# Layer two of a routed MLP behind an FFT convolution: products of the high halves first, gate factors earlier, rows of pairs fetched earlier

## The chip, the cores and the metric

The kernel runs on one core of a Trainium2 chip. The metric is device time in microseconds (us), from the launch to the end on that core; times of several executions are given with their median. A profile is one further execution, recorded by the hardware. The engines are TensorE (PE, with its weight loads as PEld), VectorE (DVE), ScalarE (ACT), GpSimd (POOL) and SyncE (SP). In this kernel SP issues nearly all transfers, and POOL issues the indirect ones that scatter rows.

## What is computed

The reference takes 8 sequences of 2496 rows of 256 numbers, convolves each with a filter by FFT (forward transform, product with the filter, inverse transform), and passes each of the 19968 resulting rows to one of 8 experts:

```
Y = irfft(rfft(x, axis=1) * F)            # 8 x 2496 x 256
logits = rows @ w_gate                    # 19968 x 8
e = argmax(logits);  g = softmax(logits)[e]
out[row] = g * (relu(row @ w1[e]) @ w2[e])   # 256 -> 1024 -> 256
```

## The kernel before

**First half.** The transforms are matrix products in fp32 in small pieces (`forward1`, `spec1`, `spec2`, `filt_`, `join`, `spec3`, `inv1`, `inv2`). For each sequence `route1` to `route6` find expert, gate and place in memory of every row, and POOL scatters the rows into `xs`, a table in device memory sorted by expert (`inv3`). Beside that the experts' weights are scaled and split into two fp16 halves, high and low, and kept in device memory as `wscr` (`w_load` to `w_out`; `w_max` is a DVE reduction of freshly loaded fp32 weights `wf`).

**Second half.** Rows are taken from `xs` in blocks of 128 of one expert. Blocks come in three stages: 7 pairs (the program's unit is a pair of blocks), 63 pairs, and single blocks. For a unit `load` fetches the rows into `xb` (4 buffers), `prep` finds the scale of each row on DVE, `split` makes the high half on ACT and the low half on DVE (both `xs`), and `turn` lets SP issue a DMA transposition into `xt` (2 buffers). `layer1` multiplies by the first weights (`wa`) into the PSUM tile `ph`; ACT makes the activation `hs` and its high half `hh`, `halves` makes the low half `hl` on DVE. `layer2` multiplies `hh` and `hl` by the second weights (`wb`) into the PSUM tile `po`, of which there is one buffer; `out_` multiplies by the gate factor `g` on ACT and `send` scatters the result. Numbers are split, so each product is three matmuls: high by high, high by low, low by high.

The weights of a unit lie in one of a few slots (`wa0`, `wa1`, `cm`, `T1` for the first layer, `wb0`, `wb1`, `bm`, `ff2` for the second; `cm`, `bm`, `T1`, `ff2` are tiles of the first half that are used again, and the views name them `cm`, `bm`, `T`, `ff`). The 63 pairs use two slots in turn. `loadw` issues about 1 MB for each unit and layer under a condition: only if the unit's expert differs from that of the slot's last unit does it move anything, at the first two pairs and at seven more. In the trace an issue that moves data takes 0.33 us or more on SP, one that is skipped 0.1 us.

**Order of the work.** Every piece is put on a list with a key, `at(key, function, ...)`; the list is sorted by key and executed, and each piece appends its instructions to the engines' queues. So a key is no time: it only sets the order in which each engine takes its instructions, and every engine then works down its own queue and waits where it must. In the pair stages a block is `d` long in keys and a pair `u = 2 d` (1.0 in the stage of 63). For a pair whose first layer starts at key z the lines at 1241 to 1253 say

```
at(max(opened(s), z - (2.1 * u if m > 1 else 2.0), OPEN + 0.1), load, k)
...
    y = max(opened(s) + 0.3, z - (2.1 if b0 < 2 else 1.35 * u if m > 1 else 1.4)) + 0.4 * d * q
    at(y, prep, b0 + q)
    at(y + 0.1, split, b0 + q)
    at(y + 0.15, turn, b0 + q)
```

where q is 0 for the pair's first block and 1 for its second. `loadw` of the first layer comes at z - 1.24 and of the second at z - 0.01, each after the slot's last reader.

Of the kernel before, what the change touches and what calls it, by code (L numbers as in the profile page):

```python
# [9 lines left out]
F32 = mybir.dt.float32  # L10
# [135 lines left out]
def tile_fft_moe(ctx, tc, x, filt_r, filt_i, w_gate, w1, w2, cst, out):  # L146
    nc = tc.nc
# [59 lines left out]
    with ExitStack() as fctx:  # L207
# [716 lines left out]
        for b in range(B):  # L924
# [5 lines left out]
            for i, f in enumerate(  # L930
# [12 lines left out]
            ):  # L943
                at(s0 + v * RT[i], f[0], b, *f[1:])
            lead = 3.2 if b < B - 2 else 2.0 if b < B - 1 else 1.3
# [25 lines left out]
        for q in range(2 * E):  # L971
            e, i = divmod(q, 2)
            z = K["w"] + K["wp"] * q
            at(z - 2.25, w_load, e, i)
            for d, f, *a in (
# [189 lines left out]
        def layer2(b, i):  # L1165
            k, j = home[b]
            m = units[k][2]
            w = wb[slot[k]]
            if i == 0:
                st[b] = (mps[2].tile([128, D], F32, name=f"po{b}", tag="pO"), *st[b][1:])  # L1170
            ps = st[b][0]
            wv = w[:, 0:4096].rearrange("p (i f d) -> p i f d", i=2, d=D)
            for f in range(4 * i, 4 * i + 4):
                c, e = divmod(f, 4 // m)
                o = (e * m + j) * 128
                for n, (q, r) in enumerate(((0, 0), (0, 1), (1, 0))):
                    nc.tensor.matmul(  # L1177
                        ps,
                        lhsT=hid[k, c][q][:, o : o + 128],
                        rhs=wv[:, r, f],  # L1180
                        start=(f == 0 and n == 0),
                        stop=(f == 7 and n == 2),
                    )
            if i:
                g0 = st[b][1]
                g = mps[0].tile([128, 1], F32, name=f"g{b}", tag="g", bufs=3)
                nc.vector.tensor_tensor(g, g0, w[:, 4096:4098].bitcast(F32), op=ALU.mult)
                st[b] = (ps, g, st[b][2])

# [47 lines left out]
        for k in range(nu):  # L1237
            s, i, m, b0 = units[k]
            z, d, _ = tau[b0]
            u = d * m  # L1240
            at(max(opened(s), z - (2.1 * u if m > 1 else 2.0), OPEN + 0.1), load, k)
            old = [j for j in range(k) if slot[j] == slot[k]]
# [6 lines left out]
            for q in range(m):  # L1249
                y = max(opened(s) + 0.3, z - (2.1 if b0 < 2 else 1.35 * u if m > 1 else 1.4)) + 0.4 * d * q  # L1250
                at(y, prep, b0 + q)
                at(y + 0.1, split, b0 + q)
                at(y + 0.15, turn, b0 + q)
            z, p = span(k)
# [72 lines left out]
```

## Time and profile before

| | us |
|---|---|
| median of 3 runs (lowest to highest) | 1317.54 (1315.71 to 1318.96) |
| the profiled execution, its own time | 1322.67 |
| its span, first to last instruction | 1320.8 |
| PE busy | 1295.3 (98%) |
| PE weight loads busy | 1116.5 (85%) |
| ACT busy | 825.7 (63%) |
| DVE busy | 748.8 (57%) |
| POOL busy | 368.2 (28%) |
| mean granted PE clock | 0.995 of full speed |

The chain that ended last runs through PE for 85% of the span and through transfers for 6%. The first half fills the span to about 450 us, the pairs run from there to about 1190 us, the single blocks to the end. Busy time is counted from the records of instructions; overlapping ones count once.

### The profile page before, as it was taken

The page shows a single profiled execution, that of the slowest core. Times are in us where ns is not written, and L with a number is a line of the kernel's source. Part 1 is how long each engine was busy: PE and PEld are TensorE (multiplying, and loading weights), DVE is VectorE, ACT ScalarE, POOL GpSimd, SP SyncE. Part 2 cuts the span into 40 slices and gives each one's busy share as a digit, 9 for nine tenths or more (in the row PEclk, how much of TensorE's full clock was granted, in tenths as well). Part 3 has the DMA queues.
Part 4 walks back from the last instruction along what each step waited for, and adds up shares of the span by engine and source line. Part 5 has one row for each costly group of instructions (what it writes and reads, how often), then busy time and mean ns, then how long its engine had stood idle before and what let it go on. Part 6 is the DMA issues. An engine that isn't in the chain of part 4 may idle for free.

```text
span 1320.8 us, 34604 instructions
## 1 busy us (share of the span) xinstructions
PE 1295.3 (98%) x12703; PEld 1116.5 (85%) x12703; DVE 748.8 (57%) x2408; ACT 825.7 (63%) x1539; POOL 368.2 (28%) x393
## 2 busy tenths in 40 slices
PE   8999999999999999999999999999999999999998
PEld 6887878878876778888888888888888888889997
DVE  2686776867866564555555545555555555544452
ACT  3566767767665676666666656666666666565564
POOL 5005345444345335422111111111211211121121
PEclk9999999999999999999999999999999999999999
DMA  8756656575636435762344342252253256548964
GB/s 216 207 149 224 204 179 224 170 232 166 202 125 190 96 94 141 216 131 74 83 115 105 106 102 77 74 137 77 74 149 78 75 139 153 144 120 231 289 164 141
DMA packets 167072, 193.99 MB, mean 147 GB/s; under 512 B 105341, under 2 KB 141785, under 8 KB 159220
## 3 DMA queue, kind: packets, MB, share of 16 engines
q1 hardware_dynamic: 146308, 147.15, 41.5%
q0 software_dynamic: 20592, 44.60, 10.8%
q8 instruction: 101, 1.65, 0.5%
q14 instruction: 71, 0.58, 0.2%
HBM read 255.61 MB, written 61.56 MB: 240 GB/s over the span
## 4 chain that ended last, share of the span: by engine, by line
PE 85%; DMA 6%; DVE 3%; issue 2%; ACT 2%; SPq 1%; POOL 0%; POOLq 0%; DVEq 0%; ACTq 0%
PE ph L1146 29%; PE po L1177 28%; PE py L696 6%; PE pi L419 5%; PE px L374 5%; PE f L289 5%; PE pg L681 3%; PE pt L356 2%; DMA xt<-xs 2%; PE plw L544 1%; DMA x<-in_x_dram 1%; DMA xb<-xs 1%; DMA ff<-in_filt_r_dram 1%; SPq L274 0%; ACT hs L1154 0%
## 5 line engine op out<-in xcount | busy, mean ns | idle before, releaser
L1162 DVE TENSOR_TENSOR hl<-hs,hh 128x512 f16<-128x512 f32 x322 | 222.0, 690 | 373.3 <-ACT hh L1156 361.2
L180 POOL DMA_INDIRECT out_dram<-ot,t x150 | 146.1, 974 | 632.5 <-ACT ot L1197 618.6
L1177 PEld LDWEIGHTS <-hh 128*128 128x128 f16 x2576 | 251.3, 98 | 34.4 <-issue 5.5
L180 POOL DMA_INDIRECT xs<-yt,dest x176 | 182.2, 1035 | 305.8 <-ACT T L298 80.3
L1154 ACT ACTIVATE hs<-ph 128x512 f32<-128x512 f32 x322 | 191.4, 594 | 80.3 <-PE ph L1146 72.6
L1156 ACT CAST hh<-hs 128x512 f16<-128x512 f32 x322 | 199.0, 618 | 10.3
L1146 PE MATMUL ph<-xt,cm 128*128 128x256 f16 (+1 forms) x1776 | 192.3, 265 | 2.5 <-DMA xt<-xs 1.3
L1146 PE MATMUL ph<-xt,T 128*128 128x256 f16 (+1 forms) x1728 | 188.2, 266 | 3.3 <-DMA xt<-xs 2.7
L1177 PE MATMUL po<-bm,hh 128*128 128x256 f16 x1104 | 184.8, 273 | 0.6 <-ACT ot L1197 0.6
L1146 PEld LDWEIGHTS <-cm 128*128 128x128 f16 x1776 | 163.8, 98 | 21.0 <-issue 3.5
L1177 PE MATMUL po<-ff,hh 128*128 128x256 f16 x1072 | 179.2, 273 | 0.0
L1146 PEld LDWEIGHTS <-T 128*128 128x128 f16 x1728 | 159.7, 98 | 22.0 <-issue 4.5
L1109 ACT ACTIVATE xs<-xb,s 128x256 f16<-128x256 f32 x161 | 81.7, 508 | 126.0 <-DVE s L1099 118.5
L1177 PE MATMUL po<-bm,hl 128*128 128x256 f16 x552 | 150.5, 273 | 0.0
L1177 PE MATMUL po<-ff,hl 128*128 128x256 f16 x536 | 146.1, 273 | 0.0
L1177 PEld LDWEIGHTS <-hl 128*128 128x128 f16 x1288 | 126.1, 98 | 14.6
L1197 ACT ACTIVATE ot<-po,g 128x256 f32<-128x256 f32 x150 | 71.1, 474 | 104.5 <-PE po L1177 81.2
L289 PEld LDWEIGHTS f<-a,x 117*128 117x128 f32 (+1 forms) x704 | 88.6, 195 | 16.5 <-issue 9.8
L289 PE MATMUL f<-a,x 117*128 117x117 f32 (+1 forms) x704 | 98.2, 282 | 1.6 <-issue 1.4
L391 DVE TENSOR_TENSOR tr<-px,ff 128x512 f32<-128x512 f32 x80 | 54.8, 684 | 78.9 <-PE px L374 61.8
L1110 DVE SCALAR_TENSOR_TENSOR xs<-xb,s,xs 128x256 f16<-128x256 f32 x161 | 77.5, 481 | 25.4 <-ACT xs L1109 25.4
L429 ACT COPY U<-pi 128x256 f32<-128x256 f32 (+1 forms) x160 | 55.2, 407 | 54.7 <-PE pi L419 54.7
(183 smaller groups left out, 1736.0 us busy)
## 6 DMA issues: line engine op xcount, KB each, us to landing
bm<-wscr SPq DMA_DIRECT2D x37, 1040.0 KB
cm<-wscr SPq DMA_DIRECT2D x37, 1024.0 KB
ff<-wscr SPq DMA_DIRECT2D x36, 1040.0 KB
T<-wscr SPq DMA_DIRECT2D x36, 1024.0 KB
xb<-xs SPq DMA_DIRECT2D x161, 130.0 KB
wb<-wscr SPq DMA_DIRECT2D x18, 1040.0 KB
wa<-wscr SPq DMA_DIRECT2D x18, 1024.0 KB
wf<-in_moe_w_dram SPq DMA_DIRECT2D x32, 512.0 KB
```

What stands on the lines that cost most here:

```text
L180: nc.gpsimd.indirect_dma_start(out=dst, out_offset=bass.IndirectOffsetOnAxis(ap=idx, axis=0), in_=src, in_offset=None, bounds_check=bound, ...
L289: nc.tensor.matmul(ps[:, n : n + m], lhsT=xt.pop((u, g))[:m], rhs=a1[:m, :m], start=True, stop=True,)
L374: nc.tensor.matmul(ps[64 * a : 64 * a + 64, i, j], lhsT=bm[:, 4 * it + 2 * j + i, 64 * a : 64 * a + 64], rhs=z[:, kk], start=True, stop=True,)
L696: nc.tensor.matmul(ps[:GP].rearrange("p g d -> p (g d)"), lhsT=dm, rhs=gt[:GP].rearrange("p g d -> p (g d)"), start=True, stop=True,)
L1109: nc.scalar.activation(xs_[:, 0], xb[:, :D], AF.Copy, scale=sc)
L1110: nc.vector.scalar_tensor_tensor(xs_[:, 1], xb[:, :D], sc, xs_[:, 0], op0=ALU.mult, op1=ALU.subtract)
L1146: nc.tensor.matmul(ps[:, n * f : n * f + n], lhsT=w[:, p : p + 128], rhs=xt[:, r, c, o1 : o1 + n], start=(a == 0), stop=(a == 5),)
L1154: nc.scalar.activation(s, ps, AF.Relu, scale=1.0 / B23)
L1156: nc.scalar.copy(hh, s)
L1162: nc.vector.tensor_tensor(hl, s, hh, op=ALU.subtract)
L1177: nc.tensor.matmul(ps, lhsT=hid[k, c][q][:, o : o + 128], rhs=wv[:, r, f], start=(f == 0 and n == 0), stop=(f == 7 and n == 2),)
L1197: nc.scalar.activation(ot, ps, AF.Copy, scale=g)
```

## The change

The diff does five things. `layer2` issues, for each half of its eight column groups, first the eight products with `hh` and then the four with `hl`, where before they alternated two and one. The gate factor `g` is formed at the start of a block's layer two instead of at its end, and the last block's result is put into a `ph` buffer instead of the only `po` buffer. In the stage of 63 pairs rows are fetched at z - 2.5 instead of z - 2.1, and the splitting and transposing of a block move closer behind its `prep` (keys y + 0.08 and y + 0.09 for the first block of a pair, y + 0.03 and y + 0.04 for the second, instead of y + 0.1 and y + 0.15). Where the pairs begin, the keys of units 0 and 1, of block 4 and of one routing step of the last sequence are set by hand. And the first fp32 weights are loaded at key 4.85, ahead of the constants at 4.9, instead of at 5.75.

```diff
--- before.py
+++ after.py
@@ -941,7 +941,7 @@
                     (route6,),
                 )
             ):
-                at(s0 + v * RT[i], f[0], b, *f[1:])
+                at(s0 + v * RT[i] - (0.15 if b == B - 1 and i == 1 else 0.0), f[0], b, *f[1:])
             lead = 3.2 if b < B - 2 else 2.0 if b < B - 1 else 1.3
 
 
@@ -971,7 +971,7 @@
         for q in range(2 * E):
             e, i = divmod(q, 2)
             z = K["w"] + K["wp"] * q
-            at(z - 2.25, w_load, e, i)
+            at(4.85 if q < 1 else z - 2.25, w_load, e, i)
             for d, f, *a in (
                 (-0.1, w_max, 0),
                 (0.1, w_max, 1),
@@ -1167,25 +1167,30 @@
             m = units[k][2]
             w = wb[slot[k]]
             if i == 0:
-                st[b] = (mps[2].tile([128, D], F32, name=f"po{b}", tag="pO"), *st[b][1:])
+                if b == NB - 1:
+                    ps = mps[1].tile([128, 512], F32, name=f"po{b}", tag="pH")[:, :D]
+                else:
+                    ps = mps[2].tile([128, D], F32, name=f"po{b}", tag="pO")
+                g = mps[0].tile([128, 1], F32, name=f"g{b}", tag="g", bufs=3)
+                nc.vector.tensor_tensor(g, st[b][1], w[:, 4096:4098].bitcast(F32), op=ALU.mult)
+                st[b] = (ps, g, st[b][2])
             ps = st[b][0]
             wv = w[:, 0:4096].rearrange("p (i f d) -> p i f d", i=2, d=D)
+            terms = []
             for f in range(4 * i, 4 * i + 4):
                 c, e = divmod(f, 4 // m)
                 o = (e * m + j) * 128
                 for n, (q, r) in enumerate(((0, 0), (0, 1), (1, 0))):
-                    nc.tensor.matmul(
-                        ps,
-                        lhsT=hid[k, c][q][:, o : o + 128],
-                        rhs=wv[:, r, f],
-                        start=(f == 0 and n == 0),
-                        stop=(f == 7 and n == 2),
-                    )
-            if i:
-                g0 = st[b][1]
-                g = mps[0].tile([128, 1], F32, name=f"g{b}", tag="g", bufs=3)
-                nc.vector.tensor_tensor(g, g0, w[:, 4096:4098].bitcast(F32), op=ALU.mult)
-                st[b] = (ps, g, st[b][2])
+                    terms.append((q, r, f, c, o, f == 0 and n == 0))
+            terms.sort(key=lambda v: v[0])
+            for q, r, f, c, o, new in terms:
+                nc.tensor.matmul(
+                    ps,
+                    lhsT=hid[k, c][q][:, o : o + 128],
+                    rhs=wv[:, r, f],
+                    start=new,
+                    stop=(f == 7 and q == 1),
+                )
 
         def out_(b):
             ps, g, t = st.pop(b)
@@ -1238,7 +1243,8 @@
             s, i, m, b0 = units[k]
             z, d, _ = tau[b0]
             u = d * m
-            at(max(opened(s), z - (2.1 * u if m > 1 else 2.0), OPEN + 0.1), load, k)
+            y = z - ((2.5 if s else 2.1) * u if m > 1 else 2.0)
+            at(max(opened(s), y - 1.3 if k == 1 else y, OPEN + 0.1), load, k)
             old = [j for j in range(k) if slot[j] == slot[k]]
             for n in range(2):
                 ahead = (
@@ -1248,9 +1254,14 @@
                 at(max(opened(s) + 0.02, t, span(k)[0] - ahead, OPEN + 0.05), loadw, k, n)
             for q in range(m):
                 y = max(opened(s) + 0.3, z - (2.1 if b0 < 2 else 1.35 * u if m > 1 else 1.4)) + 0.4 * d * q
+                v, w = (0.1, 0.15) if s == 0 or m == 1 else ((0.08, 0.09), (0.03, 0.04))[q]
+                if k == 0:
+                    y, v, w = (y, 0.03, 0.04) if q == 0 else (y + 0.14, 0.01, 0.02)
+                if b0 + q == 4:
+                    v, w = 0.33, 0.34
                 at(y, prep, b0 + q)
-                at(y + 0.1, split, b0 + q)
-                at(y + 0.15, turn, b0 + q)
+                at(y + v, split, b0 + q)
+                at(y + w, turn, b0 + q)
             z, p = span(k)
             for i in range(2 * m):
                 y = z + p * (i // 2 * 0.5 + i % 2 * 0.25 / m) if m > 1 else z + 0.25 * p * i
```

What the keys move is seen in the order of each engine's instructions.

SP in the stage of 63 pairs, before, around pair 12 (`xb26`, `xb27` are rows of pair 13; `T1` is pair 12's first-layer slot, `bm` pair 11's second-layer slot; rows of register work are left out):

```order
L1077 DMA T1_108<-wscr_58 128x4096
L1124 DMA_TRANSPOSE xt12_8405<-xs24_8377 128x4x128
L1032 TENSOR_LOAD tb1_67
L1045 DMA xb26_8443<-xs_57 128x260
L1045 DMA xb27_8445<-xs_57 128x260
L1077 DMA bm_106<-wscr_58 128x4160
L1124 DMA_TRANSPOSE xt12_8405<-xs25_8413 128x4x128
```

and now:

```order
L1032 TENSOR_LOAD tb1_67
L1045 DMA xb26_8361<-xs_57 128x260
L1045 DMA xb27_8363<-xs_57 128x260
L1124 DMA_TRANSPOSE xt12_8404<-xs24_8390 128x4x128
L1077 DMA T1_108<-wscr_58 128x4096
L1124 DMA_TRANSPOSE xt12_8404<-xs25_8428 128x4x128
L1077 DMA bm_106<-wscr_58 128x4160
```

The second transposition of a pair has moved ahead of the second-layer load and of the next rows; it now stands behind the first-layer load, which itself has moved behind the first transposition.

SP in the first half, the difference around the first expert weights (`wf`) and the constants, of which `ltf` and `small` are read by DVE between its two reductions of `wf`:

```order
 L261 DMA x_4_423<-in_x_dram 39x256
+L445 DMA wf_0_447<-in_moe_w_dram 128x1024 x2
 L852 DMA dm<-c_dm_dram 117x117
 L852 DMA small<-c_small_dram 128x64
```

The two loads of `wf` have moved ahead of the seven loads of constants.

ACT where the pairs begin, before (`xs0`, `xs1` are high halves of blocks 0 and 1, `U3`, `z78`, `gt6` and `yt6` copies of the first half's results out of PSUM):

```order
L708 COPY yt6_2_5828<-py6_4_5826 117x2x256
L429 COPY U3_121<-pi75_0_5843 128x64x3
L429 COPY U3_121<-pi75_1_5844 128x64x4
L362 COPY z78_5869<-pt78_5864 128x512
L1109 ACTIVATE xs0_5836<-xb0_5789,s0_5832 128x256
```

and now:

```order
L708 COPY yt6_2_5832<-py6_4_5830 117x2x256
L1109 ACTIVATE xs0_5840<-xb0_5789,s0_5836 128x256
L429 COPY U3_121<-pi75_0_5851 128x64x3
L429 COPY U3_121<-pi75_1_5852 128x64x4
L362 COPY z78_5877<-pt78_5872 128x512
```

The high half of block 0 has moved ahead of three copies that wait for PE.

## Rows read from the trace of the kernel before

**Rows 1.** The page's part 1, by engine: busy us, share of the span, instructions.

```profile
PE 1295.3 (98%) x12703; PEld 1116.5 (85%) x12703; DVE 748.8 (57%) x2408; ACT 825.7 (63%) x1539; POOL 368.2 (28%) x393
```

**Rows 2.** Waits of PE's weight loads, 520 to 1190, then 515 to 545 us (total, times, longest).

```profile
PEld L1146 <- issue: 8.1, 9, 2.4
...
PEld L1146 <- issue: 1.2, 2, 0.9
```

**Rows 3.** Timeline of SP's issues, 743 to 775 us: start, us taken, engine, line.

```profile
747.49 0.35 SPq L1077 DMA_DIRECT2D cm<-wscr  x1
750.21 1.20 SPq L1124 DMA_TRANSPOSE xt<-xs  x1
...
760.69 1.20 SPq L1124 DMA_TRANSPOSE xt<-xs  x1
763.05 0.94 SPq L1045 DMA_DIRECT2D xb<-xs  x2
764.57 0.33 SPq L1077 DMA_DIRECT2D bm<-wscr  x1
765.00 1.22 SPq L1124 DMA_TRANSPOSE xt<-xs  x1
```

**Rows 4.** Timeline of PE and its weight loads in the same stretch, idle time in brackets.

```profile
760.39 2.78 PE L1146 MATMUL ph<-xt,cm 128*128 128x256 f16 x24
...
773.12 1.84 PEld L1146 LDWEIGHTS <-T 128*128 128x128 f16 x15 [2.37 <-issue]
```

**Rows 5.** The chain of waits, two of its transfers: start, us until landed, what.

```profile
765.00 8.01 DMA xt<-xs
885.20 5.58 DMA xt<-xs
```

**Rows 6.** Busy by stretch: PE, PEld, DVE, ACT, POOL, PE clock, DMA share, GB/s.

```profile
57.50:60.90 3.40, 3.40 (x32) 3.23 (x32) 3.37 (x10) 1.74 (x3) 0.00 (x0) 0.50 0.84 237
426.20:429.50 3.30, 3.30 (x17) 1.81 (x13) 2.24 (x6) 0.65 (x4) 2.05 (x2) 0.50 0.95 260
774.30:777.70 3.40, 3.40 (x18) 2.42 (x17) 0.69 (x1) 1.52 (x3) 0.94 (x1) 0.50 0.61 160
```

**Rows 7.** Timeline of SP, DVE and PE, 44 to 58 us.

```profile
44.62 0.31 SPq L853 DMA_DIRECT2D ltf<-c_ltri_dram  x1
...
46.47 0.94 SPq L445 DMA_DIRECT2D wf<-in_moe_w_dram  x2
...
50.68 1.22 DVE L455 TENSOR_REDUCE wm<-wf 128x1 f32<-128x1024 f32 x1 [8.14 <-DMA wf<-in_moe_w_dram]
51.82 0.21 DVE L868 CAST ltri<-ltf 117x117 bf16<-117x117 f32 x1
...
54.46 0.68 DVE L391 TENSOR_TENSOR tr<-px,ff 128x512 f32<-128x512 f32 x1
...
57.33 0.92 PE L419 MATMUL pi<-cm,p 64*128 64x128 f32 x6 [2.40 <-DVE p L400]
```

**Rows 8.** Timeline of DVE and PE where the pairs begin, 418 to 452 us.

```profile
422.24 0.48 DVE L1110 SCALAR_TENSOR_TENSOR xs<-xb,s,xs 128x256 f16<-128x256 f32 x1 [4.05 <-ACT xs L1109]
...
424.05 1.16 PE L419 MATMUL pi<-cm,p 64*128 64x128 f32 x14 [0.72 <-DVE ti L391]
...
425.76 1.65 PE L374 MATMUL px<-z,bm 128*64 128x128 f32 x16 [0.56 <-ACT yt L708]
...
445.38 0.80 PE L544 MATMUL plw<-U,wg 128*32 128x351 f32 x8 [0.76 <-ACT U L429]
...
450.91 1.39 PE L544 MATMUL plw<-U,wg 128*32 128x351 f32 x16 [0.73 <-DVE yt L715]
```

**Rows 9.** Timeline of PE among the single blocks.

```profile
1251.28 0.38 PE L1177 MATMUL po<-wb,hh 128*128 128x256 f16 x2 [0.41 <-ACT ot L1197]
...
1312.92 0.38 PE L1177 MATMUL po<-wb,hh 128*128 128x256 f16 x2 [0.56 <-ACT ot L1197]
```

**Rows 10.** The page's costliest groups, layer two by low halves: busy, mean ns, idle before.

```profile
L1177 PE MATMUL po<-bm,hl 128*128 128x256 f16 x552 | 150.5, 273 | 0.0
```

## The prediction

> **What bounds the kernel now.** I read the page's busy shares first: PE works for 98% of the span [rows 1], so nothing but PE's own time can be long, and the question is what its idle time consists of. The waits of PE and of its weight loads answer that, then the timeline around the longest ones, then the granted clock in the stretch behind each. The reader is to see four kinds of loss. They are small, and they are all on the path that sets the end, because from the first pair on PE is never far ahead of anyone.
>
> The largest kind lies in the stage of 63 pairs: nine stalls of the first layer's weight loads, 8.1 us together, the longest 2.4 [rows 2]. Two of them (1.2 us) belong to the first pairs; the other seven come where an expert changes. The longest shows how. SP issued two blocks of rows at 763.05, a second-layer load that really moved 1 MB at 764.57, and only then, at 765.00, the second transposition of the pair that PE needed next [rows 3]. The transposition stood behind 1.3 MB and landed 8.01 us after its issue, and PE waited from 770.8 to 773.1 [rows 4, 5]. Another one landed after 5.58 us [rows 5].
>
> The second kind is the clock. After that stall PE ran at half the granted clock (1.2 instead of 2.4 GHz) for 3.4 us; the same followed the long wait at 57 us and the pair of waits at 424 us [rows 6]. Each costs half of 3.4, so 1.7 us, beyond the idle time.
>
> The third kind is in the first half: DVE stood for 8.14 us in front of its first reduction of expert weights, so that PE waited 2.40 us for a product behind it in DVE's queue [rows 7]. The fourth is four waits where the pairs begin and two among the single blocks [rows 8, 9].
>
> **The change, part by part.** The execution that I work from took 1322.67 us, of which the span is 1320.8; that is 5.1 above the median of the runs. Of the 5.1, the longest stall can explain 3.3: with its clock it cost 2.4 + 1.7, while the other six changes of expert cost (6.9 - 2.4) / 6 = 0.8 each. The remaining 1.8 I take as what this execution is slower throughout.
>
> *High halves first.* Each call of layer two still has twelve matmuls and twelve weight loads; only their order changes. A product with a low half takes 273 ns in the record, as with a high half, and no idle time stands before the low ones [rows 10]: the low halves are never late, so there is nothing to gain, and the cost is 0. If that cover went, a late low half would now stop PE four products later than before, not earlier.
>
> *Rows and transpositions of pairs.* SP's new order puts both transpositions of the next pair and the rows of the one after it ahead of the second-layer load. At the example the second transposition would go out before the load of 764.57 instead of behind it, and is needed only at 770.8. So the seven stalls go: 6.9 us, less 0.1 each because a weight load that restarts after a stall does not run a whole matmul ahead, 6.2 us. The half clock behind the longest goes with it, 1.7. The two stalls at the first pairs I leave as they are, since the first rows there still wait for the scatter; their bound is 0 to 1.2. Term: 7.9 us. What is late next is the first-layer load: it now waits in SP's queue for the first transposition, so in the example it leaves at about 752.0 (750.21 + 1.20, and 0.6 for the register work, as between 763.05 + 0.94 and 764.57) instead of 747.49 [rows 3], and the second transposition stands behind it. Both must land before the pair's first layer at 760.39 [rows 4]. Transpositions behind 1.3 MB took 5.6 to 8.0 us [rows 5]; issued at 752.4, behind 1 MB, this one lands between 758.0 and 760.4. I take 0, the near end being that of less data. The rows' buffers are free in time: the four `xb` hold two pairs, and the fetch follows directly on the older pair's second transposition.
>
> *The gate factor.* It waits only for the weights that PE also waits for. Among single blocks it now goes ahead of the low half of the next rows, which takes 0.48 on DVE as in [rows 8], so the copy out of the only `po` buffer starts earlier by that; of the 0.41 us [rows 9] I count 0.4. The last block's own PSUM buffer removes the 0.56 of the last copy [rows 9], directly at the end. Term: 1.0 us.
>
> *Where the pairs begin.* DVE waited 4.05 us for the high half of block 0, which stood on ACT behind three copies waiting for PE; behind it PE waited 0.72 and 0.56 [rows 8]. With the high half moved ahead of the copies, DVE is free some 2 us earlier, and both waits go. The wait of 0.76 came from a copy behind block 4's high half, now the other way round: one activation of 0.5 is saved. The wait of 0.73 stood on a copy of routing results that now comes a step earlier. Together 0.72 + 0.56 + 0.5 + 0.73 = 2.5, with the half clock at 426 us 4.2. The unit-1 rows that are fetched earlier are off the path, and bounded by 0.
>
> *First expert weights before the constants.* The trace does not show the constants landing behind 1 MB. The lower end is 0: DVE needs `ltf` and `small` between its two reductions, so the same bytes must have come, in another order. The upper end is the whole wait of 2.40 and its clock. SP issued `wf` at 46.47, and it was there 4.2 us later; in the new order the last thing that DVE needs is `ltf`, issued about 1.0 after its old 44.62 [rows 7]. With the same 4.2 it is there at 49.8, and DVE, which took 2.6 from this point to the product [rows 7], is 2 us early; behind 1 MB of weights it is 1 to 2 us later than that, and little is won. I take 1.4 between the two, near the first because the link was not the limit when SP issued the constants. Then 1.0 of the wait is left, and with more than half of it gone I count the 1.7 too. Term: 3.1, ends 0 and 4.1.
>
> The sum is 7.9 + 1.0 + 4.2 + 3.1 = 16.2 us. The profiled execution would take 1306.5, a median run 1.8 less, 1304.7; I say 1305.
>
> One rule speaks against three of these terms. The rows show half clock right behind three of the waits [rows 6 to 8]. The Trainium skill (TensorE: Matmul & The Clock Gate, "What's actually happening") states that the gate keeps a schedule of its own, which does not restart with the kernel. By it, idle time of the same length may bring a fall in one execution and none in the next, and with all three falls staying the sum would be 11.1. I go by the rows.
>
> **The rivals.** *The falls of the clock stay*, each hung on what idle time is left: 1304.7 + 5.1 = 1310. For it speaks that some idle time remains at the start and at the first pairs, against it that each fall in the trace stood right behind its wait. *Only the pairs and the end gain*: DVE waits for the constants as long as it did for the weights, and the waits where the pairs begin move to the next copy on ACT. Then 7.9 + 1.0 = 8.9 is won, of which 3.3 was not in the median: 1317.5 - 5.6 = 1312. Against it stands that those copies wait for PE, while what the moved high half needs was there before.
>
> *Slower.* The second transposition now stands behind the first-layer load, which leaves SP some 4.5 us later than before. If such a transposition takes over 8.0 us from its issue at 752.4, PE stalls at every change of expert at another place, and the seven removed stalls come back larger. At 2.4 + 1.7 each this is 28.7, so 1333; it decides from 8.0 us on, and 8.01 was seen, but with 0.3 MB more ahead. The Trainium skill (DMA: Bandwidth & Descriptors, "Queues, rings and completion order") says that an engine takes the descriptors of one queue in ring order; by that the transposition cannot pass the load, and the trace agrees with its 8.01 us.
>
> *No change*: the stalls turn into waits for second-layer weights, which now leave SP last. Against it: they are needed a first-layer step of 2.8 us [rows 4] after the transposition, and leave at nearly the old time. This gives 1316.
>
> **How the numbers follow.** My forecast has 0.72, the falls that stay 0.08, the gain of pairs and end alone 0.10, no change 0.06, slower 0.04. The range goes down to 1300.5 (the start at its upper end, the first pairs' 1.2 gone too, and 1.8 between runs) and up to 1312, where the second rival lies. A measurement of this kernel can tell about 0.3% from no change, 4 us: faster is below 1313.6, which holds the first three cases but for a hundredth, 0.89; same 0.07, slower 0.04.
>
> **What would show it.** In the changed profile the waits of PE's first-layer weight loads between 520 and 1190 us should fall from 8.1 to about 1.2, with no half clock there; a transposition landing after 5 us or more may remain, but behind a first-layer load and with PE not waiting. DVE's 8.14 us wait should shrink by 1 to 3, PE's wait behind it to about 1, and the four waits at the pairs' beginning should go. Idle time before products with low halves would prove the first part wrong. Waits for transpositions at the first layer's start, behind first-layer loads, would prove the slower rival.

## The result, and the profile after

The changed kernel takes 1306.35 us (median of 6 runs, 1306.16 to 1307.69); the kernel before, run beside it, takes 1319.1 us (6 runs, 1315.71 to 1321.61). The ratio is 0.9908, 95% interval 0.9894 to 0.9923: 12.8 us faster, which is 0.9% and clear of the noise. The prediction was 1305.0, range 1300.5 to 1312. The profiled execution took 1306.16 us, its span 1304.4, where the working gave 1306.5 for a profiled execution.

The page of the changed kernel, part 1 and the head of its chain, answers to [rows 1]: PE's busy time is 7.9 us less, and 99% of the span.

```profile
PE 1287.4 (99%) x12703; PEld 1112.5 (85%) x12703; DVE 749.0 (57%) x2408; ACT 821.7 (63%) x1539; POOL 368.9 (28%) x393
...
PE 90%; DVE 2%; DMA 2%; issue 2%; ACT 1%; SPq 1%; POOL 0%; POOLq 0%; DVEq 0%; ACTq 0%
```

A busy time that falls with the same 12,703 matmuls points to the clock: at half clock a matmul counts as busy for longer. The trace of the kernel before has a fourth such stretch beside the three of [rows 6], which the prediction didn't count (columns as there):

```profile
20.00:23.40 3.40, 3.40 (x24) 3.07 (x24) 2.05 (x4) 1.17 (x2) 3.19 (x6) 0.50 0.70 199
```

Half of four times 3.4 is 6.8 us, an estimate of what they added to the busy time. The mean granted clock of the changed execution is 1.000, and the stretches of it that answer to [rows 6] have no half clock:

```profile
53.00:57.00 4.00, 4.00 (x62) 3.70 (x59) 3.96 (x12) 1.52 (x4) 0.00 (x0) 1.00 0.67 216
417.00:421.00 4.00, 3.51 (x39) 2.56 (x38) 2.46 (x11) 2.68 (x7) 2.54 (x3) 1.00 1.05 231
760.00:764.00 4.00, 4.00 (x40) 3.59 (x38) 3.12 (x16) 2.23 (x6) 0.30 (x1) 1.00 0.34 95
```

To see where the 16.4 us between the two profiled spans came from, I took the start times of the same matmuls (by their number among the 12,703) in both traces. "Pairs" is matmul 5743 to 11215, that is from 600 to 1203 us of the kernel before; "end" is from there to the end of the span.

| stretch, us | before | after | won | predicted |
|---|---|---|---|---|
| first matmul to number 419 (nothing changed yet on PE) | 50.28 | 49.59 | 0.69 | 0 |
| 419 to 599: the start | 17.93 | 13.90 | 4.03 | 3.1 |
| 599 to 3925: the first half | 319.53 | 319.57 | 0 | 0 |
| 3925 to 5743: the pairs begin | 211.07 | 206.61 | 4.46 | 4.2 and the part of the first pairs |
| 5743 to 11215: the pairs | 602.91 | 595.82 | 7.09 | 7.9 |
| 11215 to the end of the span: the end | 117.88 | 117.68 | 0.20 | 1.0 |

The waits of the weight loads that answer to [rows 2], in the changed kernel from 500 to 1190 us:

```profile
PEld L1187 <- issue: 1.2, 2, 0.7
PEld L1146 <- issue: 1.2, 2, 0.9
```

The first layer's 8.1 us are down to the 1.2 of the first pairs; no wait is left at any of the seven changes of expert. The timeline of SP and of PE, answering to [rows 3, 4], shows such a change (SP, then PE):

```profile
742.58 0.35 SPq L1077 DMA_DIRECT2D cm<-wscr  x1
743.03 1.35 SPq L1124 DMA_TRANSPOSE xt<-xs  x1
...
753.24 1.19 SPq L1124 DMA_TRANSPOSE xt<-xs  x1
754.99 0.34 SPq L1077 DMA_DIRECT2D bm<-wscr  x1
756.19 0.91 SPq L1045 DMA_DIRECT2D xb<-xs  x2
```

```profile
750.57 0.60 PE L1187 MATMUL po<-bm,hl 128*128 128x256 f16 x4
751.00 2.78 PE L1146 MATMUL ph<-xt,cm 128*128 128x256 f16 x24
```

The first-layer load that moved 1 MB goes out at 742.58, the second transposition behind it at 743.03, and PE uses both from 751.00 on without idle time: they landed in at most 8.4 and 8.0 us. The load leaves 8.4 us ahead of that first layer, where it left 12.9 ahead in the kernel before (747.49 to 760.39 in [rows 3, 4]).

At the end, a line of the waits of PE (total, times, longest) and one of its timeline tell why so little was won there:

```profile
PE po L1187 <- ACT ot L1202: 2.3, 3, 1.5
```

```profile
1236.05 1.03 PE L1187 MATMUL po<-wb,hh 128*128 128x256 f16 x8 [1.49 <-ACT ot L1202]
```

The last block's 0.56 [rows 9] is gone, but the wait of 0.41, which is that of the ninth single block, grew to 1.49.

In all runs of the next section every kernel, the unchanged one too, took about 80 us longer than above, in the traces all of it between about 70 and 620 us, where PE waited for its own issue and its clock fell many times, for a reason that stays open; the ratios there stand beside the kernel before on the same chip, and the parts are read from stretches of the same matmuls.

### The profile page after: what moved, and what is told of

It is laid out like the page before. It is cut to its first block, busy times and chain, and to the rows that moved or that the text cites. A ratio compares the mean times of both kernels' runs of the same rounds, so it can differ in the third digit from the quotient of the medians.

```text
span 1304.4 us, 34542 instructions
## 1 busy us (share of the span) xinstructions
PE 1287.4 (99%) x12703; PEld 1112.5 (85%) x12703; DVE 749.0 (57%) x2408; ACT 821.7 (63%) x1539; POOL 368.9 (28%) x393
## 4 chain that ended last, share of the span: by engine, by line
PE 90%; DVE 2%; DMA 2%; issue 2%; ACT 1%; SPq 1%; POOL 0%; POOLq 0%; DVEq 0%; ACTq 0%
PE ph L1146 30%; PE po L1187 30%; PE f L289 6%; PE py L696 6%; PE pi L419 6%; PE px L374 5%; PE pg L681 3%; PE pt L356 3%; PE plw L544 1%; DMA xt<-xs 1%; DMA xb<-xs 1%; DMA ff<-in_filt_r_dram 1%; PE pgl L562 0%; POOL out_dram L180 0%; ACT U L429 0%
## 5 line engine op out<-in xcount | busy, mean ns | idle before, releaser
L1187 PE MATMUL po<-bm,hh 128*128 128x256 f16 x1104 | 143.1, 273 | 0.6 <-ACT ot L1202 0.6
L1187 PE MATMUL po<-ff,hh 128*128 128x256 f16 x1072 | 138.9, 273 | 0.0
L696 PE MATMUL py<-gt,dm 117*117 117x512 f32 x176 | 86.6, 601 | 0.0
L419 PE MATMUL pi<-cm,p 64*128 64x128 f32 (+1 forms) x1280 | 83.9, 279 | 0.0
```

The costliest lines, as they stand in the source:

```text
L419: nc.tensor.matmul(ps[a][:, e - n[a] : e], lhsT=p[q, i, j], rhs=cm[q, 4 * it + 2 * j + i, : n[a]], start=(i == 0), stop=(i == 1),)
L696: nc.tensor.matmul(ps[:GP].rearrange("p g d -> p (g d)"), lhsT=dm, rhs=gt[:GP].rearrange("p g d -> p (g d)"), start=True, stop=True,)
L1187: nc.tensor.matmul(ps, lhsT=hid[k, c][q][:, o : o + 128], rhs=wv[:, r, f], start=new, stop=(f == 7 and q == 1),)
```

## Experiments

The stretches, in us, are those of the table above, from one profiled execution of each kernel. Between kernels with the same part they scatter by about 2 us at the start, by up to 3.9 in the pairs where the seven waits are left, by up to 2.6 at the end, and by 0.13 in the pairs where no wait is left.

| kernel | ratio to before, 95% interval | start | pairs | end |
|---|---|---|---|---|
| before (as above) | 1 | 17.93 | 602.91 | 117.88 |
| high halves first alone | 0.9976 (0.9938 to 1.0015) | 17.46 | 600.07 | 118.68 |
| transpositions alone | 0.9963 (0.9936 to 0.9991) | 16.47 | 597.21 | 117.77 |
| rows alone | 0.9945 (0.9911 to 0.9979) | 18.02 | 595.71 | 117.85 |
| start alone | 0.9973 (0.9940 to 1.0005) | 14.87 | 603.92 | 118.32 |
| pairs' beginning alone | 1.0008 (0.9974 to 1.0041) | 18.01 | 602.15 | 117.23 |
| gate factor and end alone | 1.0014 (0.9981 to 1.0047) | 15.93 | 602.68 | 116.65 |
| the change again | 0.9937 (0.9905 to 0.9969) | 13.91 | 595.81 | 116.01 |
| the change, rows at the old place | 0.9971 (0.9934 to 1.0007) | 14.49 | 599.04 | 117.05 |
| the change, transpositions at the old place | 0.9950 (0.9914 to 0.9986) | 15.45 | 595.82 | 118.60 |
| second `po` | 0.9935 (0.9902 to 0.9968) | 13.82 | 595.84 | 116.02 |
| second `po` sooner | 0.9896 (0.9861 to 0.9931) | 13.82 | 595.10 | 116.02 |
| the same again | 0.9899 (0.9857 to 0.9940) | 14.45 | 595.10 | 116.02 |

**High halves first alone.** The loop over layer two as in the change, nothing else:

```diff
+                    terms.append((q, r, f, c, o, f == 0 and n == 0))
+            terms.sort(key=lambda v: v[0])
+            for q, r, f, c, o, new in terms:
```

> The kernel before with only the order of layer two's products changed (the eight products of the high halves ahead of the four with the low halves). Theory: no idle time of the matmuls in the kernel before ends in the low half of the hidden rows, so there is nothing to win: 1317 to 1320 us, ratio 0.998 to 1.002, with the seven stalls at the changes of expert still there (some 8 us of idle of the weight loads of the first layer, from 520 to 1190 us). Rival: that order shortens the wait for the hidden rows in every block, and a part of the 16.4 us that the whole change won lies here: 3 us or more, 1315 us or less.

The ratio can't be told from 1. The seven waits are all there, in the weight loads' waits from 630 to 1270 us:

```profile
PEld L1146 <- issue: 6.4, 7, 1.5
```

Theory held: the same seven took 6.9 us before. Six of them lie in the pairs' stretch (the seventh is ahead of it), and they account for its time. They sum to 4.9 us here, and to 6.1, 7.2, 7.0 and 7.4 in the four other kernels that kept them (before, start alone, pairs' beginning alone, gate factor and end alone). Take them off, and 1.7 for the one fall of the clock in the stretch of each of the first two, and 595.0 to 595.3 is left for all five; the kernels without any wait there take 595.1 to 595.8. So nothing beside the waits and the clock is left for the order of the products to win.

**Transpositions alone, rows alone.** The theory I was surest of: the second transposition's place on SP's queue is what the stalls hang on.

```diff
-                at(y + 0.1, split, b0 + q)
-                at(y + 0.15, turn, b0 + q)
+                v, w = (0.1, 0.15) if s != 1 else ((0.08, 0.09), (0.03, 0.04))[q]
+                at(y + v, split, b0 + q)
+                at(y + w, turn, b0 + q)
```

> The kernel before with only the keys of the splits and transpositions of the pairs' rows changed, in the stage of pairs: an even block's transposition is issued ahead of the pair's first-layer load, an odd one's ahead of its second-layer load; the fetch of the rows stays at 2.1 pairs ahead. Theory: the transposition's place on SP's queue is what the seven stalls hang on, so most of the 7.35 us that this stretch gave goes with it: 6 to 7.5 us, 1311.5 to 1313 us, idle of the first layer's weight loads from 520 to 1190 us near 1 instead of 8.1. Rival: the rows come too late for the earlier places, so the transposition, now ahead of the loads, holds SP until the rows have been split, the loads start later, and half or less of it is won: 3 us or less, over 1316 us.

```diff
-            at(max(opened(s), z - (2.1 * u if m > 1 else 2.0), OPEN + 0.1), load, k)
+            at(max(opened(s), z - ((2.5 if s else 2.1) * u if m > 1 else 2.0), OPEN + 0.1), load, k)
```

> The kernel before with only the rows of the pairs fetched 2.5 pairs ahead instead of 2.1, in the stages after the first; the transpositions stay behind the weight loads. Theory: the stalls stay, as the second transposition is still behind a second-layer load at each change of expert; at most the rows' own packets leave the loads' way, which is under 1 us a change: 0 to 3 us won, 1316 to 1319 us, and the idle of the first layer's weight loads from 520 to 1190 us is 5 us or more. Rival: what was late in the kernel before was the rows, and the earlier fetch alone clears the stalls: 6 us or more, 1313 us or less.

The first theory held in the main, the second fell, and its rival held. With the transpositions moved, the pairs take 597.21, 5.7 us less than in the kernel before where theory had 6 to 7.5, and no wait for a transposition is left. But four short waits ahead of layer two are, from 630 to 1270 us in the weight loads' waits:

```profile
PEld L1177 <- issue: 1.1, 3, 0.6
PEld L1177 <- DMA ff<-wscr: 0.8, 1, 0.8
```

The 0.8 is a wait for second-layer weights; the longest of the other three, 0.6, is not, as the next two runs explain.

With the rows alone the same view has no row at all, and the pairs take 595.71, as in the whole change. SP's timeline of that kernel at a change of expert says why:

```profile
844.05 1.24 SPq L1124 DMA_TRANSPOSE xt<-xs  x1
845.87 0.35 SPq L1077 DMA_DIRECT2D bm<-wscr  x1
846.32 1.41 SPq L1124 DMA_TRANSPOSE xt<-xs  x1
849.13 0.92 SPq L1045 DMA_DIRECT2D xb<-xs  x2
```

The second transposition is still behind 1 MB of second-layer weights. But the two blocks of rows, which stood between the first transposition and that load [rows 3], now come behind both. The second transposition leaves 2.27 us after the first (846.32 - 844.05) instead of 4.31 (765.00 - 760.69). Those 2.0 us are more than the average stall of 1.0 and most of the longest, 2.4; that the 0.27 MB less ahead of it made up the rest is argued, not shown.

**The same two, taken out of the change.**

```diff
-            y = z - ((2.5 if s else 2.1) * u if m > 1 else 2.0)
+            y = z - (2.1 * u if m > 1 else 2.0)
```

> The changed kernel with the pairs' rows fetched 2.1 pairs ahead again; the transpositions stay ahead of the loads. Theory, from the run with the transpositions alone: no wait for a transposition at the changes of expert, but short waits (0.3 to 0.9 us each, 2 to 3 us in all) for second-layer weights, whose load now stands behind the rows: 1.5 to 3 us over the changed kernel. Rival: the place of the transpositions is all that counts, and it is as fast as the changed kernel, under 0.5 us in such waits.

```diff
-                v, w = (0.1, 0.15) if s == 0 or m == 1 else ((0.08, 0.09), (0.03, 0.04))[q]
+                v, w = (0.1, 0.15)
```

> The changed kernel with the splits and transpositions of the pairs at their old keys again; the rows stay 2.5 pairs ahead. Theory, from the run with the rows alone, in which no stall was left from 625 to 1278 us: as fast as the changed kernel, no start of a matmul later than 0.3 us behind the end of the one ahead of it in the pairs' stretch behind its first 10 us. Rival: with the rest of the change the queue is as full as before and some of the seven stalls are back, 2 us or more of them.

The second theory held, the first in its time but only in part in its cause. Without the early rows the pairs take 599.04, 3.2 more than the change, in four waits of PE's weight loads:

```profile
PEld L1187 <- issue: 2.2, 2, 1.2
PEld L1187 <- DMA bm<-wscr: 0.8, 1, 0.8
PEld L1187 <- DMA ff<-wscr: 0.5, 1, 0.5
```

Two of the four, 1.3 us, are waits for second-layer weights. The timeline of SP in that kernel shows the rows ahead of such a load, which leaves at 844.59, 1.51 us behind their issue:

```profile
843.08 0.93 SPq L1045 DMA_DIRECT2D xb<-xs  x2
844.59 0.33 SPq L1077 DMA_DIRECT2D bm<-wscr  x1
```

The other two, 2.2 us, are something that the theory did not have. The matmuls' own waits in the same stretch (630 to 1270 us) name the copy out of the only `po` buffer:

```profile
PE po L1187 <- ACT ot L1202: 1.9, 2, 1.0
```

The timeline around the first of them shows where that copy was (SP, DVE, ACT, PE):

```profile
828.20 0.35 SPq L1077 DMA_DIRECT2D cm<-wscr  x1
...
831.69 0.96 SPq L1045 DMA_DIRECT2D xb<-xs  x2
...
836.58 0.42 DVE L1095 TENSOR_REDUCE m<-xb 128x1 f32<-128x257 f32 x1 [1.72 <-DMA xb<-xs]
...
839.91 0.45 ACT L1202 ACTIVATE ot<-po,g 128x256 f32<-128x256 f32 x1
...
840.42 1.03 PE L1187 MATMUL po<-ff,hh 128*128 128x256 f16 x8 [1.01 <-ACT ot L1202]
```

The rows' fetch of 831.69 now stands 3.5 us behind a first-layer load that moves 1 MB, and DVE waits for the rows until 836.58. ACT splits both blocks of rows ahead of the copy out of `po` (837.41 and 839.50 in the same timeline), so late rows make the copy late, and PE waits for it. In the kernel before the same fetch left 5.0 us behind that load (747.49 in [rows 3]), and no reduction waited for it:

```profile
752.53 0.92 SPq L1045 DMA_DIRECT2D xb<-xs  x2
758.55 0.41 DVE L1095 TENSOR_REDUCE m<-xb 128x1 f32<-128x257 f32 x1
```

So with the transpositions first, rows fetched at the old place are late themselves: a second reason for the early fetch. The wait of 0.6 in the kernel with the transpositions alone is of the same kind; PE waits 0.4 for the copy there.

Without the early transpositions the pairs take 595.82, as with them. Given the early rows, the transpositions' new places are worth nothing there. The two halves cover the same stalls: alone, the rows win 7.2 us of the pairs and the transpositions 5.7, together 7.1.

**Start alone.**

```diff
-            at(z - 2.25, w_load, e, i)
+            at(4.85 if q < 1 else z - 2.25, w_load, e, i)
```

> The kernel before with only the first expert's gate weights' load moved ahead of the constants at the start of the program. Theory: the stall near 54 us (2.4 to 2.7 us) goes, and with it the stretch at half clock behind it where there was one: 2.4 to 4.1 us, 1315 to 1317 us. Rival: the constants that now come second hold the same chain a step later, or the loads of the router's rows are pushed back, and nothing is won: 1318 us or more.

DVE's timeline in that kernel answers to [rows 7]:

```profile
46.97 1.22 DVE L455 TENSOR_REDUCE wm<-wf 128x1 f32<-128x1024 f32 x1 [5.27 <-DMA wf<-in_moe_w_dram]
49.85 0.22 DVE L868 CAST ltri<-ltf 117x117 bf16<-117x117 f32 x1 [1.66 <-DMA ltf<-c_ltri_dram]
```

The constants are a second, shorter wait, and PE's wait behind it shrank to 0.52. The start takes 14.87 instead of 17.93. The whole ratio's interval just reaches 1. Over all kernels of the table that wait of PE is 1.88 to 2.47 us in the six without the early load, and 0 to 0.73 in the eight with it; their starts take 15.93 to 18.02 and 13.82 to 15.45.

**Pairs' beginning alone.** The early rows of unit 1, the keys of the first blocks and of block 4, and the last router step:

```diff
+            at(max(opened(s), y - 1.3 if k == 1 else y, OPEN + 0.1), load, k)
...
+                if k == 0:
+                    y, v, w = (y, 0.03, 0.04) if q == 0 else (y + 0.14, 0.01, 0.02)
+                if b0 + q == 4:
+                    v, w = 0.33, 0.34
```

> The kernel before with only what the change does where the pairs begin: the rows of the second unit fetched 1.3 of the planner's units earlier, the splits and transpositions of the first blocks re-ordered, and the last block's router step 0.15 earlier. Theory: the four stalls from 424 to 451 us (0.72, 0.56, 0.76, 0.73 us) shrink to one, and the half-clock stretch near 426 us goes with them: 2.5 to 4.2 us, 1315 to 1317 us. Rival: the stalls were held by the weights' loads, which the early rows push back, and nothing is won: 1318 us or more.

Nothing is to be seen in the ratio, but this says little: the part lies between 388 and 506 us of the first profile, inside the 70 to 620 us named above. By the words of its expectation the rival holds. The waits of the same matmuls say more. That of 0.72 us for `ti` [rows 8] is 0.72 to 0.84 in the six kernels of the table without these keys and 0 in the eight with them, this one included; that of 0.73 for DVE's `yt` is 0.73 in all six and 0 in all eight. So the keys do end these two, 1.45 us. The other two scatter with and without the keys (for ACT's `yt` 0 to 0.56 without and 0 to 1.35 with, for `U` 0.76 to 1.54 and 0.12 to 2.40). That the part wins the whole 4.2 us of the first comparison rests on the two first traces alone.

**Gate factor and end alone.**

```diff
+                if b == NB - 1:
+                    ps = mps[1].tile([128, 512], F32, name=f"po{b}", tag="pH")[:, :D]
...
+                g = mps[0].tile([128, 1], F32, name=f"g{b}", tag="g", bufs=3)
+                nc.vector.tensor_tensor(g, st[b][1], w[:, 4096:4098].bitcast(F32), op=ALU.mult)
```

> The kernel before with only the gate factor formed before layer two and the last block's sums in another PSUM buffer. Theory: the wait of the last block for the block before it to leave PSUM goes (0.56 us), and the gate factor shortens the eviction by less than that: 0.4 to 1.0 us, 1318 to 1319 us, not to be told from no change. Rival, from the profile of the whole change, where the stretch of single blocks won 0.1 us: the gate factor puts an operation on the vector engine ahead of the split that the scalar engine waits for, and what the end wins is lost at the first single block: 0.3 us or less either way, with a wait of 1 us or more of a block's matmuls for the eviction.

The ratio is no change, as theory said. In the end stretch it takes 116.65, where the six kernels of the table with neither this part nor a part of it take 117.23 to 118.68; and of PE's waits for an eviction one is left from 1240 us on, at the last pair, so both that [rows 9] show are gone:

```profile
PE po L1183 <- ACT ot L1198: 0.6, 1, 0.6
```

So the rival fell in this run. Over all kernels of the table the last block's 0.56 is there in the six without a second buffer for it and gone in the eight that have one: that is shown. The ninth single block's wait is not settled by the gate factor: it is 0 to 0.98 in the six and 0 to 1.49 in the eight, and the kernel with the pairs' beginning alone has none either. Two later kernels with the whole part (the change with the rows and with the transpositions at the old place) take 117.05 and 118.60, much like those without it. The change again has no such wait and an end of 116.01, so the 1.49 in the first profile is no fixed price of the gate factor. In that first profile the rows' reduction on DVE came late because the rows themselves did, and the gate factor, the split and the copy out of `po` stood behind it:

```profile
1233.66 0.42 DVE L1095 TENSOR_REDUCE m<-xb 128x1 f32<-128x257 f32 x1 [3.72 <-DMA xb<-xs]
```

**The change again.** No edit.

> The changed kernel once more, unaltered, beside the other three of this group. In the first runs of this study the kernel before took about 80 us longer than in the runs ahead of the prediction, all of it ahead of 620 us, where the matmuls wait for their own issue. Theory: the parts of the change that lie behind that stretch win the same microseconds there (no stall at the changes of expert), those ahead of it win less or nothing: 7 to 14 us under the kernel before of the same group, ratio 0.990 to 0.995 if the first stretch is slow again; 0.988 to 0.993 if it isn't. Rival: in the slower state the whole gain is hidden, ratio over 0.997.

0.9937, with 7.2 us between the medians (1392.65 against 1399.83): inside what theory gave; the rival fell. Beside the first trace of the kernel before, the pairs win the same 7.1 us as in the first comparison.

**A second buffer for layer two's sums.** Every second single block's sums go to a PSUM buffer that the first half left free; then from the last block of the pairs on:

```diff
-                if b == NB - 1:
-                    ps = mps[1].tile([128, 512], F32, name=f"po{b}", tag="pH")[:, :D]
+                if b > NS and (b - NS) % 2:
+                    ps = pA.tile([128, 512], F32, name=f"po{b}", tag="pF")[:, :D]
```

> The changed kernel, with the sums of every second single block in a PSUM buffer of the pool of the first stage, so that two of them alternate (the last block among them, which so leaves the buffer that the change gave it). Theory: the matmuls' waits for an eviction, 2.3 us in the changed kernel in three places, the longest 1.5 us, go: 1304 to 1305 us, ratio to the kernel before 0.988 to 0.990, and the row of waits that names the eviction is gone or under 0.5 us. Rival: the eviction is late because its operands are, and the matmuls of the next block wait for the same thing one step later (the hidden rows): no gain on the changed kernel, 1306 us or more.

The end is 116.02, the same as the change again, and the wait of 0.56 at the last pair stays. By the rival's words it gains nothing on the changed kernel: 0.9935 beside 0.9937. This decides little, since the waits among the single blocks that it was to remove did not occur in the change again either.

```diff
-                if b > NS and (b - NS) % 2:
+                if b > NS - 2 and (b - NS) % 2:
```

> The changed kernel with two PSUM buffers for the second layer's sums from the last block of the pairs on (the run with a second buffer from the second single block on kept one wait of 0.56 us, in that place). Theory: no matmul waits for an eviction from the last pair on: 2.3 us under the changed kernel where that was undisturbed (1304 us), ratio of the two about 0.998. Rival: the last pair's second block then waits for its own hidden rows or weights, and the end comes no more than 1.7 us sooner.

Now PE has no wait from 620 us to the end of the pairs, as its busy time shows (stretch, sum, PE):

```profile
620.00:1262.00 642.00, 642.00 (x5904) 575.42 (x5902) 341.00 (x1243) 397.39 (x733) 122.44 (x127) 1.00 0.42 110
```

That is worth 0.71 us (595.81 - 595.10) to the pairs, less than the 2.3 of the theory and inside the rival's bound of 1.7, though the wait that the rival named is not there. But the ratio, 0.9896, is further below the changed kernel's than this explains, so I ran it once more.

> The kernel of the run before (two PSUM buffers for the second layer's sums from the last block of the pairs on) once more, since its time, 0.9896 of the kernel before, lay further under the changed kernel's 0.9937 than the one wait of 0.56 us that its profile lacks can explain. Theory: the rest of that difference is the scatter of the slow first stretch; from 620 us on it is 0.8 us under the changed kernel again, and the ratio comes out nearer to 0.993 (0.990 to 0.995). Rival: the second buffer helps somewhere ahead of that, and the ratio is 0.990 or less again.

0.9899: by its words the rival's number. But behind 620 us it is the 0.71 again, and the rest lies ahead of that. Most of it is the clock: the mean granted clock of the two profiled executions is 0.985 and 0.981, that of the change again 0.977, which times the spans makes 11 and 6 of the 14.2 and 9.4 us between them. What the second buffer should have to do with that no run shows, and the intervals of both and of the change again overlap. Shown are 0.71 us; the further 0.4% stay unexplained.

## Why the prediction came out

The sum came out at 16.4 us against 16.2, but this closeness is partly luck: the start gave 0.9 more than its term and 0.7 came where nothing had changed, while the end gave 0.8 less and the pairs with their beginning 0.6 less.

*High halves first: 0.* Right, by the first experiment. The "four products later" is only a mean: of a half's two chunks, the low half of the first is needed in ninth place instead of third, that of the second in eleventh instead of ninth, and the high half of the second moves forward, from seventh place to fifth. The pairs' stretches without any wait show that none of them came late.

*Rows and transpositions of pairs: 7.9.* It measured 7.1 in the pairs and some tenths more where they begin; right in size and in the picture that the stalls end and nothing takes their place. The cause is only half right. I put the stalls down to the second-layer load ahead of the transposition ("stood behind 1.3 MB") and expected the new order of the transpositions to cure them, and I gave the earlier rows no share of it. The runs show that the new order alone does end those stalls and wins 5.7 us, and that the rows' earlier fetch alone wins all of it: once it is out of the middle, a transposition may stand behind the 1 MB. As long as it stays there, moving the transposition leaves 1.4 to 3.2 us. In the weight loads' waits these are 0.8 to 1.3 for second-layer weights, which I had as the *no change* rival and priced at a full loss, and 0.6 to 2.2 for the copy out of `po`, which late rows hold up and which I had nowhere.

*Slower.* The first-layer load did leave 4.5 us later (8.4 us ahead of its use instead of 12.9), as forecast. The transposition behind it was used 7.97 us after its issue (743.03 to 751.00) without a wait; I had 8.0 as the room. The Trainium skill (DMA: Bandwidth & Descriptors, "Queues, rings and completion order") has an engine consume one queue's descriptors in ring order, but adds that a later one may finish its write before an earlier one, so it does not by itself forbid that the transposition passes the load, as I had it. No run here shows one passing.

*Gate factor and last block: 1.0.* The first profile had 0.2; later ends range from 1.9 us less than before (116.01) to 0.7 more (118.60). The 0.56 of the last block's own buffer came out as forecast. The 0.4 for the gate factor did not: the wait that it was to shorten comes and goes with the arrival of one block's rows, with the part and without it.

*Where the pairs begin: 4.2.* 4.5 in the two profiles with the first pairs' part. The waits of 0.72 and 0.73 went, there and in every later kernel with these keys. Of the wait of 0.56, which I had going together with the 0.72, 0.49 was left; the 0.76 fell to 0.12 there, but not in the later runs. The 1.7 of the clock was won in that one comparison.

*The start: 3.1.* The mis-sized term: 4.03, its upper end, in the first comparison; the wait of 2.40 went whole, and the rest is the clock. I left 1.0 of PE's wait, between the ends, since "the link was not the limit when SP issued the constants". That holds for the later of them only: the DMA share was 0.85 from 40 to 44 us and 0.33 from 44 to 47. In the profile of the change `ltf` was converted at 49.30, before the 49.8 of my early case, and PE's product starts at 54.17 with no wait. Half clock, whose 1.7 I counted in full, follows the wait in four of the six kernels without the early load: their starts take 17.46 to 18.02, the two others 15.93 and 16.47. The two rows of the changed kernel:

```profile
49.30 0.23 DVE L868 CAST ltri<-ltf 117x117 bf16<-117x117 f32 x1 [2.54 <-DMA ltf<-c_ltri_dram]
...
54.17 2.03 PE L419 MATMUL pi<-cm,p 64*128 64x128 f32 x30
```

*1.8 less for a median run.* Wrong: the changed kernel's profiled execution and its median are 0.2 apart. What the profiled execution of before had above its median I take to be waits and falls of the clock, which went with the change; that is argued from the changed kernel's runs, not shown, but a "slower throughout" is not there: the first half takes 319.53 and 319.57 us in the two traces. This step made 1306.5 into 1304.7.

*The falls of the clock.* I let each go with its wait, "right behind its wait", and had the falls that stay at 0.08. In the profiled execution all three went, but the runs show that the reason was too simple (last section). The five other executions of the changed kernel have a mean granted clock of 0.998 or 0.999, so the clock did fall in them for some us; three of their spans are still within 0.2 us of the profiled one's 1304.4.

## What to carry to other kernels

- Where a transfer lands late, look at everything that the issuing engine does between the last thing that was on time and it; here the small fetch in the middle, not the 1 MB load, was what could be moved for nothing. Move the transfer that has slack, before the one that is late.
- Undo each half of a two-part edit in both directions (alone on the old kernel, missing from the new): here this showed that the early rows alone do all the work in their stage, and that the early transpositions alone do four fifths of it and make the rows late in turn.
- Don't carry the excess of one profiled execution over the median into the forecast as a constant: count its waits and falls instead.

## What the runs showed of the hardware that I had not expected

The same wait at the same place is followed by half clock in one run and not in the next. Behind DVE's reductions at the start, first in the kernel with the transpositions alone, then with the rows alone (of each a row of PE's timeline, and the stretch behind it with columns as in [rows 6]):

```profile
57.22 1.94 PE L419 MATMUL pi<-cm,p 64*128 64x128 f32 x28 [2.47 <-DVE p L400]
```

```profile
57.20:60.60 3.40, 3.38 (x43) 3.22 (x44) 3.37 (x10) 2.01 (x5) 0.00 (x0) 1.00 0.64 214
```

```profile
57.57 1.69 PE L419 MATMUL pi<-cm,p 64*128 64x128 f32 x18 [2.43 <-DVE p L400]
```

```profile
58.50:61.90 3.40, 3.40 (x30) 3.18 (x26) 3.37 (x10) 2.43 (x5) 0.00 (x0) 0.50 0.97 331
```

2.47 us left the clock at 1.00, 2.43 brought it to 0.50. The same at a change of expert: in the kernel with the start alone the clock fell behind a wait of 2.55, in the one with the pairs' beginning alone it did not behind one of 3.11 (the same two views of each, the first here of the weight loads).

```profile
848.06 1.41 PEld L1146 LDWEIGHTS <-T 128*128 128x128 f16 x8 [2.55 <-issue]
```

```profile
847.90:851.30 3.40, 3.21 (x16) 2.25 (x17) 0.48 (x1) 1.33 (x3) 0.97 (x1) 0.50 0.40 120
```

```profile
850.17 1.87 PEld L1146 LDWEIGHTS <-T 128*128 128x128 f16 x18 [3.11 <-issue]
```

```profile
850.20:853.60 3.40, 3.40 (x32) 3.04 (x33) 1.10 (x2) 2.64 (x5) 0.97 (x1) 1.00 0.50 136
```

The Trainium skill (TensorE: Matmul & The Clock Gate, "What's actually happening") has a schedule that does not restart with the kernel, and these runs agree in that the same wait is followed by a fall in one and not in the other. I had weighed that rule against the rows and gone by the rows of one execution. What a wait of this length costs beyond itself is a chance, not a sum: 1.7 us or nothing. And a fall need not cost anything in the end: the one at 20 us put the kernel before up to 2.6 us behind the changed one, together with the longer wait ahead of it, but at matmul 140 the two are 0.06 us apart, since the changed one had waited 2.26 us for `x` by then.
